# A retention layer and a Gelu MLP on one core: the written-out list of steps in another order, some elementwise steps on other engines, and the Gelu table requested by a step of its own

## The chip, the cores and the metric

The kernel runs on one core of a Trainium2 chip. The core has five engines that each work through their own queue in order: TensorE (PE in the profile, its weight loads PEld), VectorE (DVE), ScalarE (ACT), GpSimd (POOL) and SyncE (SP), which only issues transfers. They meet through semaphores. The metric is the device time of one execution in microseconds. The median of three runs before the change is 296.26 us (296.18 to 296.48).

## What is computed

```
scores = q @ k^T / 8                       # q, k, v: 8 batches, 8 heads, 576 positions, 64 features
D[i,j] = gamma_h ** (i-j) if i >= j else 0 # gamma_h = 1 - 2**(-5-h)
x      = (scores * D) @ v                  # -> x of shape (4608, 512)
h      = x @ w_in                          # (4608, 2048)
g      = 0.5*h*(1 + tanh(c*(h + 0.044715*h**3)))
out    = g @ w_out                         # (4608, 512), float32
```

Inputs and output are float32; the kernel computes its matrix products in float16 with float32 sums.

## The kernel before, in words

The 576 positions of a batch are cut into four chunks of 128 and a tail of 64. A chunk of a batch is a *unit*; there are 40 of them, unit `u` being chunk `u % 5` of batch `u // 5`. The retention is computed chunk by chunk with a running state per head, so a unit needs its own scores, the state left by the units before it, and nothing else. The units 0, 2, 5 and 7 are *wide*: unit 0 stands for the chunks 0 and 1 together, and so on (256 positions at a time, `WIDE`, line 186). The MLP takes 512 positions at a time, `t` = 0 to 8. The first product of a `t` below 6 is made in eight pairs of 128 hidden columns and two halves of 256 positions; from `t` = 6 on, and for the second product from `t` = 1 on, the kernel uses Strassen's scheme of seven products for eight, which takes sums of blocks on VectorE before the matmuls and puts blocks together behind them.

The order of all work is written out by hand: `ORDER` (lines 17 to 123) is a list of 1,332 steps, each a letter with arguments, and the last loop of the kernel (line 1044) issues them one by one. Since the engines run in order, the list sets the order of the instructions within each engine; between the engines only data and buffers decide. The steps of the list that matter here, with the line of the work:

- `L,u,n`: SP loads q, k or v (n = 0, 1, 2) of unit u. For a wide unit it is 512 KB: q as two transfers of 128 runs of 2,048 bytes (line 198), k or v as one of 1,024 runs of 512 bytes (line 203). A tail is two transfers of 256 runs of 256 bytes (line 221), any other unit 1,024 runs of 256 bytes (line 215). All of them wait in one queue of transfers, q1 in the profile.
- `I,g` and `J,g`: POOL issues the load of an eighth of `w_in` or `w_out`, 256 packets that turn float32 into float16 on the way (line 238, queue q0). Hidden columns 0 to 511 need `I` 0 and 1, the next 512 `I` 2 and 3, and so on. `i` and `j` do nothing for these.
- `q`, `k`, `v` (lines 424, 439, 267, 269): float16 copies of a unit's q and v times powers of gamma, and of k. The last letter names the engine: `v` VectorE, `a` ScalarE, `g` GpSimd.
- `D,u` (line 483): q and k of a unit transposed by a transfer; `t,u,q|k,pool` (line 493): the same on TensorE for the first units, and `y` copies the result out of PSUM.
- `X`, `Y`, `m`, `R`, `B`, `x` (lines 619, 636, 644 and 691, 677, 529 to 574, 586 to 599): keys times values, scores, scores times the mask, outputs of a wide unit, the same of other units, and the copy of the output into `xT`, the input of the MLP.
- `a`, `o`, `z` (lines 711 to 731): the running state, its decay, and its float16 copy `sz` for the matmuls.
- `N,t,fc,half` and `F,t,fc,half` (lines 757, 765): eight matmuls of the first product, and their Gelu on ScalarE. `A`, `l`, `f`, `s`, `U` are the same in Strassen's form. `N` and `A` take turns in two PSUM banks, so an `N` waits until the Gelu of the one two places before it has read its bank.
- `O`, `W` and `e`, `V`, `H`, `T`: the second product, and for Strassen's form its sums and its blocks; two other PSUM banks. `S`, `P`, `E`, `Q`: stores of the results, and the last 128 rows in three column parts.
- `K,n`: n matmuls on the identity matrix with no use but to keep TensorE at work (line 1003). `Z`, `g`, `c`: constant tables and zeros.
- `w`: one Gelu of a [128, 1] tile whose result nobody reads (line 1008). ScalarE must load a table when it changes from exponentials to Gelu.

Buffers turn in rings: seven for the loaded pages, four for the float16 q and k, four for the transposed ones, six for `sz`.

Of the kernel before, what the change touches and what calls it, by code (L numbers as in the profile page):

```python
# [28 lines left out]
N,1,4,0 O,0,5 N,1,14,0 F,1,4,0 m,7,0 N,1,2,0 L,12,2 O,0,1 X,7 Y,7,1 F,1,14,0 F,1,2,0 L,15,1 k,9,a  # L29
O,0,6 O,0,2 N,1,10,0 F,1,10,0 q,9,g O,0,3 L,11,2 N,1,6,0 D,9 F,1,6,0 m,7,1 Z,0,g k,11,a a,7,1 O,0,7  # L30
e,0,0,v a,8,1 z,6,1,v O,0,12 T,1,0,v N,1,0,0 e,0,1,a F,1,0,0 z,8,1,g z,7,1,v N,1,8,0 O,0,13 L,10,1
N,1,12,0 R,7 B,9,-1 H,1,0,3,v v,10,v F,1,8,0 x,8 O,0,8 L,11,0 L,12,1 O,0,14 j,5,v F,1,12,0 v,11,v
T,1,1,v q,11 k,10,g x,7 O,0,15 N,1,6,1 H,1,0,1,v L,12,0 D,10 N,1,8,1 O,0,9 F,1,6,1 T,2,0,v v,9,v
O,0,10 e,0,3,a T,3,0,v S,0,0 N,1,14,1 F,1,8,1 H,1,0,2,v m,9 L,14,1 B,10,9 k,12,a D,11 T,2,1,v O,0,11
a,10,0 a,10,1 e,0,2,v N,1,12,1 L,13,2 F,1,14,1 L,13,0 x,9 N,1,10,1 m,10 F,1,12,1 T,3,1,v z,10,0,g
B,11,10 q,12,g W,1,0,1 S,0,3 v,13,v a,11,0 V,1,0,0,a a,11,1 x,10 v,12,v W,1,0,6 L,14,0 F,1,10,1
N,1,2,1 o,11,1 q,13,g F,1,2,1 T,4,0,v D,12 W,1,0,2 L,16,1 V,1,0,1,v N,1,4,1 N,1,0,1 S,0,2 V,1,0,2,a
z,11,0,v F,1,4,1 z,10,1,g j,2,v m,11 S,0,1 N,2,0,0 B,12,11 q,14 a,12,0 H,1,0,4,v k,15,g F,1,0,1
F,2,0,0 W,1,0,7 L,15,0 L,14,2 N,2,8,0 T,4,1,v N,2,4,0 V,1,0,3,v H,1,1,1,v L,13,1 z,12,0,g x,11
k,16,g H,1,1,2,v W,1,0,4 W,1,0,5 F,2,8,0 L,17,0 a,12,1 N,2,6,0 L,17,1 V,1,0,5,v L,19,0 F,2,4,0  # L40
k,13,g D,13 V,1,0,4,v F,2,6,0 m,12 N,2,14,0 v,14,v F,2,14,0 W,1,1,1 z,11,1,g V,1,1,0,a W,1,0,3
V,1,0,6,v L,16,0 N,2,10,0 F,2,10,0 k,14,g W,1,1,6 V,1,1,1,v N,2,12,0 z,12,1,v L,16,2 B,13,12 x,12
L,15,2 v,15,g D,14 q,15 W,1,1,2 H,1,1,3,v m,13 N,2,2,1 V,1,1,2,a W,1,1,7 F,2,12,0 N,2,2,0 V,1,1,3,v
k,17,a W,1,1,4 W,1,1,5 a,13,0 a,13,1 S,1,0 z,13,0,a q,19 q,17 q,16 F,2,2,1 S,1,1 D,15 L,17,2 F,2,2,0
L,18,0 N,2,8,1 B,14,13 N,2,12,1 L,20,0 F,2,8,1 V,1,1,5,v F,2,12,1 N,2,6,1 V,1,1,4,v W,2,0,1 x,13
N,2,10,1 F,2,6,1 m,14 H,2,0,1,v H,2,0,2,v z,13,1,v N,2,0,1 D,16 V,2,0,0,a L,24,1 B,15,14 H,1,1,4,v
a,15,0 L,18,2 H,2,0,3,v W,1,1,3 a,15,1 F,2,0,1 m,15 V,1,1,6,v q,18,g v,17,v F,2,10,1 N,2,4,1
N,2,14,1 L,18,1 L,19,1 x,14 v,16,g F,2,14,1 W,2,0,2 z,15,0,g B,16,15 W,2,0,6 F,2,4,1 x,15 k,19,g
a,16,0 N,3,8,0 V,2,0,1,v V,2,0,2,a a,16,1 F,3,8,0 o,16,1 z,16,0,v m,16 W,2,0,7 D,17 V,2,0,3,v L,23,1
v,18,g N,3,10,0 k,18,g F,3,10,0 L,24,0 L,20,1 N,3,4,0 F,3,4,0 z,15,1,g W,2,0,4 z,16,1,v B,17,16  # L50
L,21,0 N,3,0,0 q,20 V,2,0,5,v a,17,0 L,25,1 L,19,2 D,18 H,2,0,4,v L,20,2 S,1,2 W,2,0,5 N,3,12,0
W,2,1,1 F,3,0,0 m,17 q,21,g H,2,1,3,v V,2,0,4,v H,2,1,1,v F,3,12,0 k,20,g W,2,0,3 N,3,14,0 N,3,6,0
S,1,3 F,3,14,0 V,2,0,6,v V,2,1,0,a L,22,1 N,3,2,0 L,21,1 D,19 H,2,1,2,v W,2,1,6 a,17,1 x,16 z,17,0,g
B,18,17 F,3,6,0 a,18,0 H,2,1,4,v D,20 x,17 a,18,1 W,2,1,2 N,3,8,1 F,3,2,0 m,18 N,3,2,1 i,2,g
z,18,0,a v,19,v V,2,1,2,a L,22,0 W,2,1,7 z,18,1,g V,2,1,1,v F,3,8,1 v,20,g N,3,4,1 F,3,2,1 k,22,v
k,21,v L,25,0 N,3,12,1 W,2,1,5 F,3,4,1 z,17,1,a B,19,18 H,3,0,3,v V,2,1,3,v L,23,0 N,3,0,1 H,3,0,1,v
x,18 F,3,12,1 W,2,1,4 m,19 V,2,1,5,v k,23,g N,3,10,1 W,3,0,1 V,2,1,4,v L,24,2 B,20,19 W,2,1,3
F,3,0,1 L,22,2 x,19 D,21 F,3,10,1 a,20,0 q,23,g N,4,10,0 N,3,14,1 V,3,0,0,a V,2,1,6,v F,4,10,0
H,3,0,2,v W,3,0,6 S,2,0 N,3,6,1 F,3,14,1 S,2,1 F,3,6,1 W,3,0,2 q,22,g a,20,1 L,21,2 D,22 N,4,6,0
m,20 V,3,0,2,a z,20,0,v H,3,0,4,v N,4,12,0 V,3,0,1,v v,21,g L,27,0 F,4,6,0 W,3,0,7 k,24,v B,21,20  # L60
W,3,0,5 N,4,4,0 F,4,12,0 x,20 z,20,1,g V,3,0,3,v H,3,1,3,v W,3,0,4 L,23,2 v,22,v k,25,a v,24,g
a,21,0 V,3,0,4,v m,21 F,4,4,0 S,2,2 N,4,0,0 F,4,0,0 a,21,1 V,3,0,5,v z,21,0,g v,23,g B,22,21 L,28,0
q,25,g N,4,2,0 m,22 L,26,0 x,21 W,3,1,1 q,26,g N,4,14,0 V,3,1,0,a L,30,2 D,23 W,3,0,3 o,21,1 L,27,2
L,26,1 H,3,1,1,v L,26,2 H,3,1,2,v q,24,g W,3,1,2 F,4,2,0 L,29,1 V,3,0,6,v F,4,14,0 V,3,1,2,a N,4,4,1
a,22,0 v,27,v z,22,0,a S,2,3 D,24 W,3,1,6 S,3,0 F,4,4,1 L,28,1 H,3,1,4,v N,4,8,0 z,21,1,v D,25
a,22,1 F,4,8,0 N,4,14,1 W,3,1,7 k,26,a H,4,0,1,v z,22,1,v B,23,22 N,4,6,1 V,3,1,1,v V,3,1,3,v L,25,2
F,4,14,1 a,23,0 W,3,1,5 F,4,6,1 V,3,1,4,v W,3,1,4 N,4,12,1 i,1,g a,23,1 z,23,0,g z,23,1,g F,4,12,1
x,22 W,3,1,3 N,4,0,1 F,4,0,1 q,27 L,28,2 m,23 N,4,2,1 H,4,0,2,v B,24,23 q,28,g N,4,8,1 V,3,1,5,v
F,4,2,1 H,4,0,3,v L,29,0 V,3,1,6,v L,27,1 x,23 F,4,8,1 W,4,0,1 v,25,g N,4,10,1 m,24 V,4,0,0,a D,26
H,4,1,3,v k,28,v F,4,10,1 N,5,2,0 B,25,24 k,27,g S,3,1 F,5,2,0 H,4,1,1,v q,29 a,25,0 L,31,1 a,25,1  # L70
# [1005 lines left out]
```

## Time and profile before

| | |
|---|---|
| median of 3 runs | 296.26 us |
| the profiled execution, first to last instruction (span) | 293.9 us |
| time outside the span, taken against the median | about 2.3 us |
| TensorE at work | 280.3 us, 95% of the span, 4,064 matmuls |
| VectorE, ScalarE, GpSimd at work | 216.6, 150.1, 109.6 us |
| granted TensorE clock, mean | 1.000 |
| read from and written to HBM | 36.70 MB and 9.44 MB |

A page of the profile gives for each engine its busy time, then groups of equal instructions with their mean duration and what ended the idle time before them. The busy time of TensorE is modelled at the ends of its matmuls, so its gaps are read from the starts of successive matmuls. The transfers have a view of their own: for a stretch of time it tells how many packets each queue moved.

### The profile page before, as it was taken

To read this page: it belongs to the slowest core of one execution; us is meant where nothing else is said; L and a number is where in the kernel's file an instruction comes from. 1 tells how busy PE (TensorE), PEld (TensorE's weight loads), DVE (VectorE), ACT (ScalarE), POOL (GpSimd) and SP (SyncE) were. 2 spreads that over 40 slices of the span, in tenths; PEclk is the share of its full clock that TensorE was granted. 3 is DMA by queue.
4 is the path that set the end of the run, shared out by engine and by line. 5 is a ranking of instruction groups with operands and counts; after the bars stand their busy time and mean duration, and the time that the engine had idled before them with its cause. 6 is when DMAs were issued, how large, how long until landed. Compare 5 with 4: busy or idle time off the path is not lost.

```text
span 293.9 us, 9639 instructions
## 1 busy us (share of the span) xinstructions
PE 280.3 (95%) x4064; PEld 235.2 (80%) x4064; DVE 216.6 (74%) x447; ACT 150.1 (51%) x289; POOL 109.6 (37%) x168
## 2 busy tenths in 40 slices
...
GB/s 212 283 236 250 217 220 211 214 179 162 248 142 228 178 186 220 230 206 210 23 235 214 196 166 178 187 204 153 131 195 208 75 205 7 36 8 102 74 25 121
DMA packets 136428, 49.79 MB, mean 169 GB/s; under 512 B 118208, under 2 KB 130880, under 8 KB 136384
## 3 DMA queue, kind: packets, MB, share of 16 engines
...
HBM read 36.70 MB, written 9.44 MB: 157 GB/s over the span
## 4 chain that ended last, share of the span: by engine, by line
PE 86%; POOL 5%; DMA 4%; DVE 3%; issue 1%; ACT 0%; POOLq 0%; ACTq 0%
PE bank L860 30%; PE bank L757 27%; PE bank L957 12%; PE bank L783 6%; DMA w_in_sb<-in_moe_w_in_dram 4%; PE sk L553 2%; PE x L529 2%; POOL w_in_sb L238 2%; PE sk L563 1%; PE x L574 1%; PE bank L987 1%; DVE pages L817 1%; POOL wide L269 1%; PE bank L493 1%; PE x L677 1%
## 5 line engine op out<-in xcount | busy, mean ns | idle before, releaser
L757 PE MATMUL bank<-xT,w_in_sb 128*128 128x256 f16 x768 | 94.4, 273 | 2.1 <-DMA w_in_sb<-in_moe_w_in_dram 2.1
L765 ACT ACTIVATE gT<-bank 128x512 f16<-128x512 f32 x96 | 56.7, 598 | 61.5 <-PE bank L757 59.7
L757 PEld LDWEIGHTS <-w_in_sb 128*128 128x128 f16 x768 | 73.8, 98 | 13.7 <-DMA w_in_sb<-in_moe_w_in_dram 2.7
L860 PEld LDWEIGHTS <-ssum 128*128 128x128 f16 x480 | 46.3, 98 | 6.5 <-issue 0.8
L269 POOL CAST sz<-s 64x256 f16<-64x256 f32 x48 | 24.4, 509 | 66.2 <-DVE s L713 45.9
L860 PE MATMUL bank<-tsum,ssum 128*128 128x256 f16 x360 | 46.0, 273 | 0.6 <-DVE ost L817 0.6
L860 PEld LDWEIGHTS <-gT 128*128 128x128 f16 x360 | 34.8, 98 | 4.5 <-issue 0.2
L424 POOL TENSOR_TENSOR qk<-pages,dec 128x512 f16<-128x512 f32 (+1 forms) x20 | 22.2, 1122 | 32.9 <-DMA pages<-in_q_dram 17.2
L860 PE MATMUL bank<-w_out_sb,gT 128*128 128x256 f16 x240 | 31.1, 273 | 0.0
L817 DVE TENSOR_TENSOR ssum<-gT 128x1024 f16<-128x1024 f16 x30 | 23.9, 798 | 3.9 <-ACT gT L765 3.5
L424 POOL TENSOR_TENSOR v<-pages,dec 128x512 f16<-128x512 f32 (+1 forms) x20 | 20.6, 1030 | 15.3 <-DMA pages<-in_v_dram 10.4
L817 DVE TENSOR_TENSOR ost<-u,bank 128x256 f32<-128x256 f32 x45 | 18.1, 416 | 9.5 <-PE bank L860 9.4
L817 DVE TENSOR_TENSOR ssum<-gT,ssum 128x1024 f16<-128x1024 f16 x30 | 23.4, 782 | 0.2
L691 DVE TENSOR_TENSOR ret<-sk,mask 128x512 f16<-128x512 f32 (+1 forms) x32 | 19.8, 618 | 4.3 <-PE sk L563 4.0
L957 PEld LDWEIGHTS <-pages 128*128 128x128 f16 x192 | 18.4, 98 | 2.8 <-issue 0.3
L957 PE MATMUL bank<-pages 128*128 128x256 f16 x144 | 20.3, 273 | 0.3 <-ACT pages L267 0.3
L783 PE MATMUL bank<-w_out_sb,gT 128*128 128x512 f16 x80 | 19.1, 380 | 0.0
L817 DVE TENSOR_TENSOR u<-u,bank 128x256 f32<-128x256 f32 x30 | 12.4, 415 | 8.7 <-PE bank L860 5.0
L713 DVE TENSOR_TENSOR s<-s,sk 128x256 f32<-128x256 f32 x36 | 14.9, 415 | 5.0 <-PE sk L563 4.0
L593 ACT ACTIVATE xT<-x 128x512 f16<-128x512 f32 (+1 forms) x25 | 14.3, 578 | 8.0 <-PE x L574 8.0
L817 DVE TENSOR_TENSOR hc<-hc,bank 128x512 f32<-128x512 f32 x21 | 14.4, 684 | 5.0 <-PE bank L957 2.3
L267 ACT COPY hc<-bank 128x512 f32<-128x512 f32 x19 | 11.1, 585 | 12.5 <-PE bank L957 12.4
(114 smaller groups left out, 425.8 us busy)
## 6 DMA issues: line engine op xcount, KB each, us to landing
...
```

The costliest lines, as they stand in the source:

```text
L267: nc.scalar.copy(out=o, in_=i)
L269: (nc.vector if eng == "v" else nc.gpsimd).tensor_copy(out=o, in_=i)
L424: eng.tensor_tensor(out=out, in0=s["raw"][:, i, 0:n], in1=dec[:, i // 2, s["j"], 0:n].unsqueeze(2).to_broadcast([128, n, D]), op=ALU.mult,)
L593: nc.scalar.activation(out=xT[:, :, o : o + G * (b - a)].rearrange("c p (h s) -> c p h s", s=G), in_=x[:, a:b].rearrange("c h p s -> c p h ...
L691: nc.vector.tensor_tensor(out=ret[:, :, 0:n], in0=now["two"][:, :, 0, 0:n], in1=mask.unsqueeze(1).unsqueeze(1).to_broadcast([128, 2, n, G] ...
L713: nc.vector.tensor_tensor(out=s32, in0=state[0], in1=kv, op=ALU.add)
L757: nc.tensor.matmul(hps[:, i, :], w_in_sb[:, ct, 128 * (fc + i) : 128 * (fc + i) + 128], xT[:, ct, TB * t % XR + lo : TB * t % XR + hi], st ...
L765: nc.scalar.activation(out=gTs[t][:, fc : fc + TB // (hi - lo), lo:hi], in_=h.pop((t, fc, lo)), func=AF.Gelu_apprx_tanh, bias=0.0, scale=1.0,)
L783: nc.tensor.matmul(ops[t, tcc], gTs[t][:, ft, 128 * tcc : 128 * tcc + 128], w_out_sb[:, ft, :], start=(ft == 0), stop=(ft == NFC - 1),)
L817: (nc.vector if eng == "v" else nc.gpsimd).tensor_tensor(out=out, in0=a, in1=b, op=op)
L860: nc.tensor.matmul(p["ps", bank][:, HN * col : HN * col + HN], a[:, k], b[:, k], start=(k == 0 and i in (1, 6)), stop=(k == HK - 1), skip_ ...
L957: nc.tensor.matmul(p["ps", bank][:, n], w[:, c, 128 * n : 128 * n + 128], x[:, c], start=(n == 0 and c == 0 and i in (1, 2, 5)), stop=(c = ...
```

## The change

All 1,332 steps are still there, with the same arguments but for the engine of some of them, and they stand in another order. Counted over both lists:

- The engine changes in 106 steps. `z`: 31 on GpSimd, 15 on VectorE and 10 on ScalarE become 24, 17 and 15. `k`: 19, 8 and 9 become 13, 7 and 16. `q`: 20 on GpSimd and 16 on VectorE become 15 and 21. `v`: 20 and 16 become 23 and 13. Of `V`, ten move from ScalarE to VectorE (20 and 85 after it), of `l` three net from VectorE to ScalarE (33 and 39), and one or two each of `e`, `E`, `y` and `Z`.
- At the start, the loads of SP stood as k0, q0, v0, k2, q2, v2, k4, q4, q5, k5, v5, v4, k9, k7, q7, v7. They become k0, v0, q0, q2, k2, v2, q4, k4, v4, k5, q5, v5, q7, k7, v7, k9. The loads of `w_in` stood as 2, 7, 1, 0, 3, 6, 4, 5 and become 1, 6, 0, then GpSimd's `c` and `q,2,g`, then 7, 2, 3, 5, 4. Between the first three loads of `w_out` and the other five GpSimd now does `q,7,g`.
- 19 of the 36 filler matmuls of `K` stood ahead of the first transpose; 23 do now.
- `w` stood in the middle of the list, behind 84 of the 96 steps `F`. It now stands behind `z,1,1,a` and ahead of the first `N` and `F`.
- `pair` gives the buffers of a pair of row blocks by the number of the pair in its `t`, not by the count of pairs so far. In both lists the pairs come in turn (0, 1, 0, 1, ...), so each gets the buffers that it had.

```diff
--- before.py
+++ after.py
@@ -15,111 +15,111 @@
 ORDER = """
-L,0,1 Z,1,v L,0,0 I,2,g L,0,2 L,2,1 L,2,0 Z,2,g q,0 k,0,g I,7,g K,4 K,4 K,4 K,3 K,4 t,0,q,h L,2,2
-L,4,1 c t,0,k,h I,1,g v,0,v X,0 y,0,k,v I,0,g I,3,g a,0,1 y,0,q,v Z,3,v k,2,g K,4 K,1 Y,0,1 t,2,k,o
-m,0,1 z,0,1,a I,6,g K,4 Y,0,0 a,1,1 q,2 L,4,0 K,4 t,2,q,h m,0,0 y,2,k,a y,2,q,v I,4,g K,1 R,0 I,5,g
-x,0 Y,2,1 L,5,0 x,1 i,4,v K,3 N,0,2,0 N,0,0,0 g o,1,1 m,2,1 L,5,1 Z,4,g v,2,v F,0,2,0 N,0,12,0 Y,2,0
-F,0,0,0 z,1,1,v N,0,4,0 L,5,2 X,2 k,4,g Z,5,v q,4 F,0,12,0 F,0,4,0 t,4,k,o a,2,1 t,4,q,o a,3,1
-y,4,q,a N,0,8,0 L,4,2 z,2,1,g L,9,1 N,0,10,0 F,0,8,0 k,5,g m,2,0 L,7,1 R,2 F,0,10,0 y,4,k,v B,4,-1
-q,5 x,3 x,2 N,0,14,0 L,7,0 t,5,q,o N,0,0,1 L,7,2 J,1,g F,0,14,0 N,0,6,0 y,5,q,v J,3,g t,5,k,o
-F,0,0,1 m,4 j,1,v J,0,g L,9,0 v,5,v J,2,g L,9,2 F,0,6,0 N,0,8,1 L,10,0 N,0,12,1 k,7,v X,5 y,5,k,a
-F,0,8,1 z,3,1,g F,0,12,1 v,4,v Y,5,0 a,5,1 m,5,0 a,6,1 N,0,4,1 N,0,6,1 F,0,4,1 q,7 F,0,6,1 t,7,k,o
-y,7,k,a N,0,2,1 J,5,g J,4,g N,0,14,1 F,0,2,1 J,6,g L,10,2 B,-1,4 F,0,14,1 x,4 Y,5,1 t,7,q,h y,7,q,a
-J,7,g m,5,1 N,0,10,1 v,7,v F,0,10,1 z,5,1,g R,5 x,5 Y,7,0 o,6,1 x,6 O,0,0 O,0,4 q,10,g L,11,1
...
+Z,2,g j,0,v K,4 K,4 K,3 K,4 K,3 Z,1,g I,1,g K,1 L,0,1 k,0,a L,0,2 K,4 I,6,g t,0,k,h y,0,k,a I,0,g
+v,0,v X,0 L,0,0 q,0 t,0,q,h y,0,q,a K,4 g L,2,0 a,0,1 z,0,1,a a,1,1 Y,0,1 m,0,1 c L,2,1 k,2,v K,4
+L,2,2 q,2,g Y,0,0 m,0,0 L,4,0 t,2,q,h y,2,q,a t,2,k,o y,2,k,v R,0 x,0 L,4,1 x,1 L,4,2 Y,2,1 Z,3,v
+v,2,v o,1,1 z,1,1,a K,1 K,4 w N,0,0,0 F,0,0,0 X,2 m,2,1 N,0,2,0 F,0,2,0 a,2,1 z,2,1,a Y,2,0 I,7,g
+N,0,14,0 F,0,14,0 I,2,g q,4 t,4,q,o N,0,12,0 F,0,12,0 L,5,1 Z,4,g a,3,1 m,2,0 R,2 x,3 k,4,v t,4,k,o
+I,3,g N,0,6,0 Z,0,g I,5,g y,4,q,v x,2 y,4,k,v F,0,6,0 B,4,-1 z,3,1,v N,0,4,0 F,0,4,0 m,4 N,0,12,1
+L,5,0 N,0,6,1 F,0,12,1 v,4,v F,0,6,1 I,4,g N,0,8,1 F,0,8,1 q,5 N,0,10,0 F,0,10,0 N,0,8,0 F,0,8,0
+k,5,g t,5,k,o y,5,k,a L,5,2 v,5,v L,7,0 N,0,0,1 F,0,0,1 Z,5,v L,7,1 J,1,g J,0,g t,5,q,o y,5,q,a
+N,0,14,1 X,5 a,5,1 F,0,14,1 a,6,1 J,2,g Y,5,0 m,5,0 N,0,4,1 F,0,4,1 k,7,a N,0,2,1 F,0,2,1 q,7,g
+B,-1,4 L,7,2 Y,5,1 m,5,1 t,7,q,h x,4 L,9,1 t,7,k,o y,7,k,a z,5,1,g N,0,10,1 F,0,10,1 R,5 x,5 x,6
+y,7,q,v Y,7,0 O,0,4 m,7,0 J,3,g L,9,0 O,0,0 N,1,2,0 F,1,2,0 L,9,2 v,7,v N,1,4,0 Y,7,1 J,5,g o,6,1
+X,7 F,1,4,0 N,1,6,0 F,1,6,0 L,10,0 L,10,2 J,4,g T,3,0,v N,1,14,0 F,1,14,0 O,0,1 q,9 a,7,1 T,1,0,v
+a,8,1 L,10,1 N,1,10,0 L,11,0 F,1,10,0 J,7,g N,1,12,0 k,9,a O,0,5 O,0,6 D,9 J,6,g T,1,1,v T,2,1,v
+O,0,2 N,1,8,0 L,11,1 z,7,1,a F,1,8,0 z,6,1,v F,1,12,0 L,12,1 O,0,7 O,0,3 e,0,0,v e,0,1,a L,13,0
+N,1,0,0 q,10 O,0,12 O,0,13 O,0,14 F,1,0,0 m,7,1 R,7 x,8 H,1,0,3,v v,9,g k,10,g D,10 B,9,-1 v,10,v
...
-W,8,0,5 H,8,0,4,v f,8,3,2 P,2 V,8,0,4,v W,8,0,4 V,8,0,5,v W,8,0,3 O,8,8 E,2,v V,8,0,6,v S,8,0 O,8,9
-O,8,10 O,8,11 P,0 e,8,2,a Q,2 S,8,1 E,0,v P,1 S,8,2 E,1,a Q,0 Q,1 i,7,v
+V,8,0,3,v W,8,0,5 V,8,0,4,v W,8,0,4 V,8,0,5,v W,8,0,3 f,8,2,2 P,2 V,8,0,6,v S,8,0 E,2,v O,8,8 S,8,1
+O,8,9 O,8,10 O,8,11 e,8,2,a S,8,2 P,0 E,0,a Q,2 Q,0 P,1 E,1,a Q,1
 """
...
@@ -834,8 +834,7 @@
         if (t, pr) not in pairs:
             if not tsum:
                 sum_tiles()
-            n = len(pairs)
-            pairs[t, pr] = dict(s=[ssum[4 * (n % 2) + i] for i in range(4)])
+            pairs[t, pr] = dict(s=[ssum[4 * pr + i] for i in range(4)])
         return pairs[t, pr]
 
     def sum_a(t, pr, i, eng):
```

More of the change, by code (lines that the diff above doesn't have):

```diff
@@ L29 @@
[L29 to L70, printed above, removed]
```

138 lines of the change are left out of this document (88 added, 50 removed).

## The prediction

> **What bounds the kernel now.** I read the page's header first, then TensorE's starts in the timeline, then busy time in five stretches.
>
> ```profile
> span 293.9 us, 9639 instructions
> PE 280.3 (95%) x4064; PEld 235.2 (80%) x4064; DVE 216.6 (74%) x447; ACT 150.1 (51%) x289; POOL 109.6 (37%) x168
> ...
> 4.50 5.92 PE L1003 MATMUL bank<-ident 128*128 128x512 f16 x19 [4.50 <-DVE ident L364]
> ...
> 21.30 1.91 PE L757 MATMUL bank<-xT,w_in_sb 128*128 128x256 f16 x16
> 24.85 1.05 PE L757 MATMUL bank<-xT,w_in_sb 128*128 128x256 f16 x8 [1.64 <-DMA w_in_sb<-in_moe_w_in_dram]
> ...
> 41.86 0.45 PEld L493 LDWEIGHTS <-wide 128*128 128x128 f16 x8
> ```
>
> The first `N` starts at 21.30, the next but one waits for `w_in` until 24.85. Two `N` take 1.75 us where nothing waits (the pieces of the chain of waits), so one is 0.873.
>
> ```profile
> core 0: us, PE busy (x) PEld busy (x) DVE busy (x) ACT busy (x) POOL busy (x), PEclk, DMA share, GB/s
> ...
> 21.30:29.28 7.98, 5.88 (x94) 4.41 (x93) 5.50 (x11) 3.70 (x6) 1.01 (x3) 1.00 1.19 249
> 29.28:41.87 12.59, 12.59 (x231) 11.12 (x228) 8.82 (x12) 9.06 (x15) 8.78 (x13) 1.00 1.05 218
> 41.87:224.00 182.13, 182.05 (x2846) 156.03 (x2841) 136.13 (x262) 94.86 (x187) 78.68 (x103) 1.00 0.95 188
> 224.00:229.00 5.00, 3.95 (x35) 3.12 (x33) 4.97 (x9) 3.43 (x7) 2.85 (x3) 1.00 0.81 199
> ```
>
> From 29.28 to 224 TensorE never stops; at 224 to 229 it loses 1 us to a VectorE that is busy for 4.97 of 5. By its starts it waits 2.4 us in all between 29.28 and the end, structural changeovers left out. So the change can win only ahead of 29.28 and in these 2.4 us, and it can lose anywhere. The start is bound by transfers:
>
> ```profile
> q0 software_dynamic: 645, 0.63, 73.9%
> q1 hardware_dynamic: 645, 0.55, 43.0%
> ...
> q1 hardware_dynamic: 997, 0.57, 119.2%
> ...
> q1 hardware_dynamic: 8351, 2.09, 100.8%
> ```
>
> The first two lines are the transfer view for 16 to 21 us: while POOL's queue has weights to move, the two queues move one packet each in turn, 129 per us each. From 36 to 44 us it is 1,119 and 1,114 packets, 140 per us. Alone (7.5 to 9.4 us, packets of 512 bytes) SP's queue moves 997 in 1.9 us, 525 per us; packets of 256 bytes alone (48 to 58) go at 835. So a wide k or v, 1,024 packets, takes 1.5 (27.4 to 28.9 us: 1,021 packets) to 1.95 us alone and 7.3 to 7.9 us beside the weights, and a tail's 512 packets of 64 KB each half cost half as much as a whole wide tensor there.
>
> **The start, step by step.** Loads of SP are issued far ahead, so their order decides.
>
> (1) POOL does two memsets (0.53 each, line 390) ahead of its first `I`, issued at 6.43 before; now at 7.5. The first packets of that queue came 3.3 us after the issue (30 of them in the window 9 to 10); now at 10.8. By then SP's queue, alone at 300 GB/s from 1.9 on, has moved k0, v0, q0, q2 (2.1 MB, 7.0 us) and k2 (1.9).
>
> (2) The 2,048 packets of `w_in` then need 2,048/140 = 14.6 to 2,048/129 = 15.9 us, plus about 0.3 for the gap in which POOL does `c` (1.45, line 395) and `q,2,g`. That multiply is new on POOL; bounds 1.27 (VectorE's, line 439) and 2.4 (twice POOL's 1.20 for half the size); I take 2.2, nearest to POOL's own row. `w_in` ends at 25.7 to 27.2. In that time SP's queue moves as many packets: v2, q4, k4, and little more. Before, it had passed q5 and k5 too, because the weights came in single issues (6.43, 9.03, 11.14) with gaps: 4,014 of its packets against 2,142 from 10 to 28 us.
>
> (3) The matmuls meanwhile. 23 fillers now stand ahead of the first transpose, at 4.50 + 8 x 0.427 + 15 x 0.216 = 11.16 (before: 19, 10.26). The chain from there: `y,0,k` on ScalarE 11.75 to 12.76 (1.01, line 267), `y,0,q` to 13.8, `Y,0,1` at 14.0 (14.75 before), masks 14.5 to 17.9 (2 x 1.22 and a cast of 0.94), `R,0`, `x,0` and `x,1` to 19.75, fillers, first `N` at 20.4, 0.9 earlier. Columns 0 to 511 of `w_in` have landed by 18 (768 packets from 10.8). v2 lands at about 18.9 and holds up VectorE: `v,2`, `o,1,1`, then `z,1,1,a` until 21.5 on ScalarE, and behind it `w` with its table (1.28, the row of line 765) until 23.0. So the request comes too late to hide the table: the first Gelu ends at 23.6 and the third `N` waits 0.8 us. It cost nothing before either, since TensorE stood for `w_in` until 24.85.
>
> (4) Ahead of `t,7,k` the new list has exactly the matmuls that stood ahead of `t,7,q` before (15 `N`, the same `t`, `X`, `Y`, `R`, `B`), and the same ones follow. So 41.87, the old start of that step, is the yardstick. Nothing else waiting, TensorE gets there at 20.4 + 17.7 of work + 0.8 = 38.9: 3.0 us won.
>
> (5) But k7 isn't there. After `w_in` SP's queue still has v4 (0.6 alone), k5 (1.7), q5 (1.8 at 295 GB/s), v5 (1.7), q7, k7. k5 ends at 28.0 to 29.5 and lands 0.7 later (k0: 4.2, landed 4.93). POOL casts it (1.04) and only then issues three loads of `w_out`, whose packets come 2.7 us later, at 32.4 to 33.9. q7 ends at 33.5 to 35, and k7 meets 768 packets of `w_out`: 5.5 to 6 us shared, the rest alone. k7 ends at 38.6 to 41.5 (the upper end if the next five loads follow at once), lands 0.7 later; `k,7,a` on ScalarE is new at this size: bounds 1.01 (its copy of 1,024 in float16) and 1.24 (twice 0.618), I take 1.1. `t,7,k` starts at 40.5 to 43.4; I take 41.7. Queued behind `k,7,a` on ScalarE are `F,0,2,1`, `x,4` and `y,7,k`; TensorE itself waits 2.8 us. Start: 0.2 us won (from 1.4 won to 1.5 lost); the 3.0 are given back. Before, k7 was ahead of `w_out`: VectorE cast it at 35.49, without a wait.
>
> ```profile
> 29.07 1.04 POOL L269 CAST wide<-pages 128x1024 f16<-128x1024 f32 x1
> 30.05 2.88 POOL L238 DMA_DIRECT2D w_out_sb<-in_moe_w_out_dram  x4
> ...
> 35.49 0.94 DVE L269 CAST wide<-pages 128x1024 f16<-128x1024 f32 x1
> ```
>
> v7 and the later `J` have 2 us or more in hand by the same count.
>
> **The engines.** Steps times their rows' means: POOL 108.9 to 94.6, ScalarE 159.4 to 168.9 (with `w`), VectorE 232.4 to 232.6. ScalarE and POOL stay far below 267.3 us of matmuls, so their shares lie beside TensorE's work. VectorE decides by stretch. From `W,4,0,1` to the first `A` of t = 6 it now has 31.5 us of steps to 29.5 of matmuls (before 32.6 to 33.0); around `A,7,0` 16.1 to 13.9 (before 14.5 to 13.1, and there the 1.5 us of waits at 224 to 229 are). Means overlap by 7% (232.4 listed, 216.6 busy), so the two stretches have 29.3 to 29.5, all but full (before 30.3 to 33.0), and 15.0 to 13.9 (before 13.5 to 13.1). What is late next there are `V` and `l`, thus the banks of `W` and `A`. Price: 0.7 more in the second, 0.5 in the first, 1.2 us; bounds: minus 2.4 (all old waits gone) and plus 2.5 (both excesses unhidden). Ten `V` moved to VectorE (0.416 for 0.372) are in these sums. `pair` changes nothing, and the tail (store behind the last copy, 3.1 us) stays.
>
> Sum: 296.26 - 0.2 + 1.2 = 297.2 (the profiled span 293.9 to 294.9; the 2.3 us around it stay).
>
> **Rivals.** (a) k7 comes in time: if POOL's loads of `w_out` start so late, or packets pass so fast alone, that k7 is past by 37. Then 3.0 less 0.5 stay, with 0.5 lost late: 294.3. Against it: k5's landing lets `w_out` go before q7 is through in every count above. (b) The start is even, and VectorE in the late stretches is no worse, since 14.3 us less of POOL stand beside it: 295.3 to 296.6, say 296.0. For it: ssum took 1.42 beside a POOL multiply, 0.69 elsewhere. Against: late POOL steps are the same 18.3 us. (c) TensorE waits so long for k7 that its clock falls. The first eight fillers came 0.42 apart, later ones 0.216: 8 x 0.21 = 1.65 us for a cold engine. A wait of 2.06 us at 11.5 cost nothing (five fillers in 1.25). It needs a longer wait than that; from one of 3.4 us (`t,7,k` at 42.3, 0.6 later than taken) 297.8 + 1.65 = 299.5. The upper third of (5) reaches that far, and a wait of that length need not be enough: 0.12.
> The Trainium skill ("TensorE: Matmul & The Clock Gate", section "What's actually happening") states that the clock halves after an idle window of about 3.4 us; no wait of this trace is long enough to show it, and the row of 2.06 us agrees. By that rule a long wait gives 299.5, without it 297.8.
>
> **How the numbers follow.** Chances: forecast 0.44, (a) 0.17, (b) 0.27, (c) 0.12. No change means within 0.2%, 295.67 to 296.85, about what a measurement can tell. Faster: (a) 0.17 and half of (b), 0.30. Same: 0.12 of (b), 0.05 of the forecast, 0.17. Slower: 0.53. The range, 294.2 to 299.8, takes in (a) and most of (c); the forecast's own is 296.0 to 298.6.
>
> **What would show it.** Right: first `N` at 20 to 20.6, third `N` waiting for a Gelu, TensorE idle 2 to 3.5 us ahead of a transpose (line 493) at 40.5 to 43.4 with ScalarE's cast waiting for k7, then no wait until `W,4`; VectorE full around 165 to 195 and 225 to 240. Wrong: that transpose near 39, or TensorE stopping at places not named.

## The result, and the profile after

The changed kernel takes 304.54 us (median of 4 runs, 302.24 to 306.25) against 296.37 us (4 runs, 296.18 to 297.55): a ratio of 1.026 with a 95% interval of 1.021 to 1.032. A second set of six runs gave 305.17 us. It is slower by about 8 us, far more than the 1 us forecast. Where a run of one variant lies over 1.5% above its fastest, the figures below are of that variant's other runs alone. The page's header and engines:

```profile
span 303.6 us, 9626 instructions
PE 282.8 (93%) x4064; PEld 236.4 (78%) x4064; DVE 217.3 (72%) x455; ACT 159.3 (52%) x302; POOL 95.4 (31%) x147
```

The span has grown by 9.7 us (303.6 against 293.9; the profiled run, 305.61, is one of the longer ones). The matmuls are the same, and VectorE has 0.7 us more to do: the time is waiting. Where, the busy time by stretch shows (stretch, its length, then busy time and count of TensorE, its weight loads, VectorE, ScalarE, GpSimd; granted clock; mean share of the DMA engines; GB/s), first of the changed kernel, then of the kernel before:

```profile
19.60:27.10 7.50, 6.35 (x128) 5.02 (x127) 5.20 (x11) 6.23 (x12) 1.50 (x2) 1.00 1.18 240
27.10:40.25 13.15, 12.77 (x195) 10.72 (x195) 6.49 (x10) 8.70 (x14) 6.45 (x10) 1.00 1.14 250
40.25:101.40 61.15, 61.15 (x865) 48.35 (x866) 38.95 (x68) 32.49 (x63) 20.01 (x26) 1.00 0.99 197
101.40:168.00 66.60, 59.67 (x1000) 52.92 (x998) 46.97 (x99) 32.88 (x64) 20.48 (x25) 1.00 1.03 185
168.00:196.00 28.00, 27.62 (x460) 24.72 (x459) 24.28 (x49) 12.25 (x25) 8.17 (x11) 1.00 0.78 171
196.00:257.00 61.00, 57.43 (x842) 50.03 (x840) 54.34 (x104) 35.89 (x70) 24.47 (x34) 1.00 0.64 131
```

```profile
102.00:168.00 66.00, 65.92 (x1054) 58.61 (x1052) 45.99 (x92) 32.72 (x64) 30.24 (x38) 1.00 1.00 192
196.00:250.00 54.00, 52.95 (x811) 46.82 (x809) 48.90 (x96) 37.53 (x75) 23.60 (x32) 1.00 0.66 143
```

From 40 to 101 us TensorE runs through. Then it is idle for 6.9 of 66.6 us, where the kernel before lost 0.1 of 66.0; and for 3.6 of 61.0 us from 196 on, against 1.1 of 54.0. By the starts of successive matmuls, less each step's usual duration, the waits of over 0.1 us behind 101 us add up like this (a wait is dated here and below by the start of the step that it falls in or follows):

| waits of TensorE | before | after |
|---|---|---|
| start: `t,7,k` (before: `t,7,q`) begins at | 41.87 | 40.25 |
| 101 to 166 us | 0.2 | 7.7 |
| 168 us to the end | 2.2 | 5.9 |

So, before rounding, 1.6 us are won at the start, 7.4 lost in the middle, 3.8 late: 9.6 of the 9.7 us. The start (timeline, one line per run of like instructions: start, length, engine, line, operation, operands, count, in brackets the idle time ahead of it and what ended it):

```profile
19.60 1.04 PE L757 MATMUL bank<-xT,w_in_sb 128*128 128x256 f16 x8
22.70 1.03 PE L757 MATMUL bank<-xT,w_in_sb 128*128 128x256 f16 x8 [0.25 <-ACT gT L765]
27.07 0.83 PE L757 MATMUL bank<-xT,w_in_sb 128*128 128x256 f16 x6 [0.90 <-DMA w_in_sb<-in_moe_w_in_dram]
...
20.66 1.28 ACT L1010 ACT_TABLE_LOAD   x1
39.15 1.04 ACT L267 CAST wide<-pages 128x1024 f16<-128x1024 f32 x1 [0.60 <-DMA pages<-in_k_dram]
...
40.24 0.45 PEld L493 LDWEIGHTS <-wide 128*128 128x128 f16 x8 [0.55 <-ACT wide L267]
```

The first `N` is early, the table load sits nearly hidden under it, `w_in` holds `N,0,6,0` until 27.07, and `t,7,k` does wait for k7's cast, but only 0.55 us. In the middle, the chain of waits (start, length, what) runs through SP's transposes:

```profile
140.90 0.29 PE bank L859 x2
141.19 5.49 DMA qkT<-qk
146.73 0.32 PE sk L563 x16
...
150.77 0.25 PE bank L757 x3
151.03 5.06 DMA qkT<-qk
156.13 0.26 PE sk L563 x8
```

These are `D,23` and `D,24`: TensorE reaches `B,23` at 145.2 and `B,24` at 154.1, and stops 1.06 and 1.70 us in them. Why they are so late, VectorE's timeline tells:

```profile
104.49 0.75 DVE L817 TENSOR_TENSOR ost<-u,bank 128x256 f32<-128x256 f32 x2 [3.66 <-DMA out_dram<-ost]
...
146.87 0.29 DVE L269 CAST qk<-pages 128x256 f16<-128x256 f32 x1 [1.12 <-DMA qkT<-qk]
149.06 0.42 DVE L817 TENSOR_TENSOR ost<-u,bank 128x256 f32<-128x256 f32 x1 [0.68 <-PE bank L859]
149.40 0.42 DVE L424 TENSOR_TENSOR qk<-pages,dec 128x256 f16<-128x256 f32 x1
```

`k,24` takes the tile that unit 23 had, so it stands until `D,23` has landed; `q,24`, whose page landed at 112.6, stands in VectorE's queue behind it and behind a `V` that waits for TensorE; only then can SP issue `D,24`. The first line is another stop, the longest (3.05 us at 101.4): a `V` needs a result tile whose store, `S,0,2`, SP issued at 98.7. The stops look like SP's: late stores, late transposes. That was the first theory.

One number of all units puts it in order. From the issue of `D,u` to the start of `B,u`, units 14 to 31, the kernel before has 9.8 us (median; least 7.8), the changed one 7.0 (least 3.1; six units under 5.5). A transpose lands 4.3 us after its issue (median; 3.7 in the kernel before; up to 5.9). The attention of units 18 to 31 stands 4 to 13 us of matmuls earlier in the changed list (the steps' durations summed over each list up to `B,u`), while the transfers are no earlier: 29.69 MB had moved by 140 us before, 29.63 after. And GpSimd's casts, 42 to 200 us, stand waiting for pages (engine, what for: total, times, longest; before, then after):

```profile
POOL qk L424 <- DMA pages<-in_q_dram: 15.5, 2, 13.1
POOL v L424 <- DMA pages<-in_v_dram: 10.4, 2, 6.6
POOL qk L269 <- DMA pages<-in_k_dram: 1.6, 2, 1.4
```

```profile
POOL qk L269 <- DMA pages<-in_k_dram: 23.4, 4, 9.3
POOL v L424 <- DMA pages<-in_v_dram: 22.5, 5, 9.4
POOL qk L424 <- DMA pages<-in_q_dram: 14.6, 3, 8.1
POOL qk L269 <- DMA pages<-in_q_dram: 4.7, 1, 4.7
```

27.5 us have become 65.2.

### The profile page after: what moved, and what is told of

Its sections match the earlier page's. It is cut to its first block, busy times and chain, and to the rows that moved or that the text cites. A ratio compares the mean times of both kernels' runs of the same rounds, so it can differ in the third digit from the quotient of the medians.

```text
span 303.6 us, 9626 instructions
## 1 busy us (share of the span) xinstructions
PE 282.8 (93%) x4064; PEld 236.4 (78%) x4064; DVE 217.3 (72%) x455; ACT 159.3 (52%) x302; POOL 95.4 (31%) x147
## 4 chain that ended last, share of the span: by engine, by line
PE 37%; DVE 14%; DMA 9%; issue 3%; SPq 1%; ACT 0%; POOL 0%; DVEq 0%
PE bank L859 17%; PE bank L956 8%; DMA qkT<-qk 7%; PE bank L757 6%; DVE ssum L817 3%; DVE pages L817 2%; DVE s L713 1%; DMA pages<-in_v_dram 1%; DVE ost L817 1%; DVE sz L269 1%; DVE ret L691 1%; PE bank L986 1%; PE sk L563 1%; PE bank L783 1%; DVE qk L424 1%
## 5 line engine op out<-in xcount | busy, mean ns | idle before, releaser
L424 POOL TENSOR_TENSOR v<-pages,dec 128x512 f16<-128x512 f32 (+1 forms) x23 | 23.9, 1041 | 38.2 <-DMA pages<-in_v_dram 30.9
L269 POOL CAST sz<-s 64x256 f16<-64x256 f32 x38 | 19.3, 508 | 39.7 <-DVE s L713 30.1
L817 DVE TENSOR_TENSOR ssum<-gT 128x1024 f16<-128x1024 f16 x30 | 22.9, 765 | 0.4 <-ACT gT L974 0.3
L817 DVE TENSOR_TENSOR ssum<-gT,ssum 128x1024 f16<-128x1024 f16 x30 | 22.2, 740 | 0.3
L956 PE MATMUL bank<-pages 128*128 128x256 f16 x144 | 21.2, 273 | 1.1 <-DVE pages L817 0.7
L424 POOL TENSOR_TENSOR qk<-pages,dec 128x512 f16<-128x512 f32 (+1 forms) x13 | 13.6, 1053 | 20.7 <-DMA pages<-in_q_dram 20.3
L267 ACT COPY hc<-bank 128x512 f32<-128x512 f32 x21 | 12.3, 585 | 12.9 <-PE bank L956 12.7
L269 POOL CAST qk<-pages 128x512 f16<-128x512 f32 (+1 forms) x12 | 8.7, 731 | 29.0 <-DMA pages<-in_k_dram 23.4
```

The source lines that it names most:

```text
L267: nc.scalar.copy(out=o, in_=i)
L269: (nc.vector if eng == "v" else nc.gpsimd).tensor_copy(out=o, in_=i)
L424: eng.tensor_tensor(out=out, in0=s["raw"][:, i, 0:n], in1=dec[:, i // 2, s["j"], 0:n].unsqueeze(2).to_broadcast([128, n, D]), op=ALU.mult,)
L817: (nc.vector if eng == "v" else nc.gpsimd).tensor_tensor(out=out, in0=a, in1=b, op=op)
L956: nc.tensor.matmul(p["ps", bank][:, n], w[:, c, 128 * n : 128 * n + 128], x[:, c], start=(n == 0 and c == 0 and i in (1, 2, 5)), stop=(c = ...
```

## The experiments

Times are medians; the kernel before stood between 296.6 and 297.0 us beside them. In the experiments' files the list takes five lines less, so line 262 there is 267 of the changed kernel. The changed kernel's own runs lie 2 to 4 us apart, so differences of under 1.5 us between its variants say little.

| run | us | against the kernel before, 95% |
|---|---|---|
| the changed kernel / once more (e18) | 304.54 / 305.17 | 1.021 to 1.032 / 1.020 to 1.029 |
| e1 store early | 304.68 | 1.021 to 1.034 |
| e2 15 transposes early / e3 both | 314.71 / 311.45 | 1.055 to 1.062 / 1.043 to 1.054 |
| e16 two transposes early / e17 and q casts (five of six runs) | 307.94 / 305.70 | 1.031 to 1.042 / 1.021 to 1.032 |
| e5 few store rows / e6 the same, before | 302.17 / 296.27 | 1.012 to 1.020 / 0.997 to 0.999 |
| e7 before's order / e8 after's order, letters swapped | 306.43 / 341.14 | 1.028 to 1.039 / 1.144 to 1.154 |
| e9 attention later | 316.85 | 1.061 to 1.069 |
| e13 fifth cast tile (two of four runs) / e14 three q casts on GpSimd | 301.80 / 302.86 | 1.012 to 1.022 / 1.017 to 1.028 |
| e10 before, then after / e11 after, then before | 301.10 / 302.18 | 1.009 to 1.019 / 1.011 to 1.019 |
| e4 start of after / e12 longer / e15 longer, `w` late | 295.71 / 294.82 / 295.13 | 0.993 to 0.998 / 0.991 to 0.996 / 0.993 to 0.997 |

### Is it the late store?

```diff
-... N,2,12,0 S,0,3 i,0,a N,2,12,1 ... W,1,1,7 H,1,1,4,v S,0,2 B,14,13 ...
+... N,1,12,1 S,0,3 H,1,0,1,v ... W,1,0,2 S,0,2 N,1,4,1 ...
```

> The changed list with two steps moved alone: S,0,3 and S,0,2 (stores of the first token block's results) stand about 6 us of matmuls behind the copies e,0,3 and e,0,2 that fill them, instead of 28. Theory A (the 3.05 us stop of TensorE ahead of product W,2,0,1 is a result buffer waiting for S,0,2, which SP issues only at 98.7): that stop is gone, 304.5 falls by about 3 to 301.5 (300.5 to 302.5), and VectorE has no wait for a store near 101. Rival B (VectorE and the banks are the limit from here on, the store only the last to come): the stop stays, or comes back a few steps later, and the time stays within 1 us of 304.5.

304.68 us: no gain. The stop at 101.4 is gone, but now ScalarE stands for a page 12 us ahead of it, and TensorE 2.15 and 0.77 us behind ScalarE's Gelus (timeline, ScalarE, then TensorE):

```profile
90.63 0.62 ACT L262 CAST qk<-pages 128x512 f16<-128x512 f32 x1 [3.19 <-DMA pages<-in_k_dram]
91.16 0.59 ACT L760 ACTIVATE gT<-bank 128x512 f16<-128x512 f32 x1
...
91.80 1.03 PE L752 MATMUL bank<-xT,w_in_sb 128*128 128x256 f16 x8 [1.99 <-ACT gT L760]
```

The page is k14's: SP issued `L,14,1` at 86.87 instead of 84.18. But the changed kernel run once more (e18, below) has the same stops, 1.80 and 0.77 us, and none at 101, with both stores in their old places and `L,14,1` at 85.15 (its timeline):

```profile
91.23 1.03 PE L757 MATMUL bank<-xT,w_in_sb 128*128 128x256 f16 x8 [1.64 <-ACT gT L765]
```

So the stop at 101.4 comes and goes without an edit, and no gain hangs on it; that the store's move delayed the page is not shown.

### Is it the late transposes?

```diff
-... q,14,g ... D,12 v,12,g B,12,11 ... V,3,0,4,v F,4,6,0 L,29,0 q,24 ... U,3,1 D,24 B,24,23 ...
+... k,12,g D,12 q,14,g ... v,12,g B,12,11 ... q,24 D,24 N,4,4,1 ... U,3,1 B,24,23 ...
```

> The changed list with 15 of the 31 DMA transposes D moved forward, to 4 to 6 us of matmuls ahead of the attention step B that reads them (as they stand, eight are right ahead of it), never ahead of their own casts; nothing else. Theory A (a late transpose in SP's queue stops TensorE at line 563): the stops at 145.2, 154.1, 224.2 and 244.1 (1.06, 1.70, 0.63, 0.60) go, TensorE's waits for qkT fall from 3.8 us to under 1, and the time falls by 3 to 4 to about 301 (300 to 302). Rival B (VectorE is the limit from 140 on: what TensorE no longer waits for a transpose it waits for VectorE's banks): the waits at line 563 go but those at lines 859 and 956 grow, the time stays above 303. Rival C (SP stands at the early transposes, loads and stores behind them come later): new waits for pages or ost, 304 or more.

> Both moves together. Theory A: the gains add, 304.5 - 3 - 3.5 = 298 (297 to 299.5); what stays above the kernel before is VectorE's stops of the late stretch. Rival B: no more than the better one of the two alone, 301 or more.

314.71 and 311.45 us: 10 and 7 us worse. Waits at line 563 fell from 3.8 to 1.1 us as expected, but SP now stands at transposes whose casts aren't done (from 18.1 to 26.2 us at casts of q on VectorE alone), the loads behind them come later, and `B,31` starts at 203.0 instead of 192.3. Now the same with only two moved:

```diff
-... L,27,2 D,22 B,22,21 ... v,23,v D,23 B,23,22 ... q,24 N,4,4,1 ... U,3,1 D,24 B,24,23 ...
+... L,27,2 D,22 D,23 B,22,21 ... v,23,v B,23,22 ... q,24 D,24 N,4,4,1 ... U,3,1 B,24,23 ...
```

> The changed list with two of its transposes moved alone: D,23 forward right behind D,22, and D,24 right behind q,24; 4 and 14 steps of TensorE's and other engines' order stand as they were. Theory (the stops at 145.2 and 154.1 are these two, standing in SP's queue behind loads that could wait): D,23 is issued near 136 instead of 141.2 and lands before B,23; k,24 does not wait, q,24 is cast at 148, D,24 issued at once and landed by 153; the stops 1.06 and 1.70 lose 2 to 2.5 us, 302 to 302.6. Rival G (the queue is full, so what goes ahead of the loads takes their place: their pages come later, and the stop comes one or two units on): 304 or more, with a stop at B,25 to B,28.

307.94 us, the rival. The stops at 145.2 and 154.1 go; 0.70 us come at `B,22` and 0.90 at a product that waits for a `V` of ScalarE. And SP, free earlier, comes to `D,24` early and stands there 4.7 us for `q,24`; `L,27,0` behind it is issued at 157.7 instead of 155.7. VectorE reaches `q,27` and has no page, and TensorE waits for the state that VectorE was to make next (timeline, VectorE, TensorE):

```profile
163.48 1.46 DVE L419 TENSOR_TENSOR qk<-pages,dec 128x512 f16<-128x512 f32 x1 [3.74 <-DMA pages<-in_q_dram]
164.86 0.41 DVE L708 TENSOR_TENSOR s<-s,sk 128x256 f32<-128x256 f32 x1
...
165.32 0.43 PE L548 MATMUL sk<-v,qk 64*64 64x64 f16 x16 [3.34 <-DVE s L708]
```

Behind that stop the granted clock fell (stretches of the same run, columns as above; the last but two is the granted clock):

```profile
160.00:165.00 5.00, 1.99 (x22) 1.69 (x19) 1.52 (x2) 1.96 (x5) 4.18 (x5) 0.90 1.03 138
165.00:167.00 2.00, 1.60 (x52) 1.38 (x53) 2.00 (x5) 0.77 (x2) 1.27 (x2) 0.50 0.38 74
167.00:169.00 2.00, 2.00 (x12) 1.39 (x11) 1.43 (x5) 0.82 (x2) 0.00 (x0) 0.50 0.45 90
171.00:174.00 3.00, 3.00 (x78) 2.70 (x76) 1.98 (x6) 1.45 (x4) 0.14 (x1) 1.00 1.42 199
```

By an estimate from these rows, some 5.5 us of work at 0.50 cost up to 2.7 us more. In e2 the stop at 101 grew to 4.65 us and the clock was at 0.50 from about 106 to 112.5, and again from 146.8 to 150.2.

### Is it bytes, the four cast tiles, or VectorE's casts?

In e5 and e6 the 12 stores write 8 of 128 rows:

```diff
-        stores[t, tcc] = out[r0 : r0 + 128, :], ost
+        few = 8 if (t, tcc) in FEW else 128
+        stores[t, tcc] = out[r0 : r0 + few, :], ost[0:few]
```

> The changed kernel with 12 stores (S,0,2, S,0,3, all of blocks 1 and 2, S,3,0 and S,3,1; issued from 86 to 178 us) writing 8 of their 128 rows; 120 rows of each of these tiles are left unwritten. Every instruction keeps its place and its wait; 2.95 of 49.8 MB are not moved. Theory T (the DMA engines are full, share 1.0, until 168 us, and the changed list puts the attention steps of units 18 to 31 earlier by 4 to 13 us of matmuls than the list before, so their pages and transposes come too late): 2.9 MB are 14 us of transfer at 205 GB/s, spread over 90 us, so the pages land 2 to 14 us sooner and most of the 6.4 us of stops between 101 and 160 goes: 304.6 falls by 4 to 7, to 298 to 300.5. Theory Q (SP stands at a store or a transpose and all behind it waits, bytes do not matter): within 1.5 us of 304.6. Theory V (VectorE is the limit from 100 on): within 1.5 us too, with the waits at lines for the banks grown.

> The kernel before with the same 12 stores writing 8 of 128 rows. All theories: TensorE has no wait over 0.25 us between 42 and 223 there, so within 0.5 us of the kernel before, 296.4 to 297.4. It is the control: a gain of more than 1 us here would say that the shorter stores help by another way than pages that come sooner.

302.17 us, 2.4 less than the changed kernel and short of the 4 to 7 expected; the control gains 0.5. The 3.05 us stop goes and 1.65 come at 88.7 and 90.4, as 2.57 do in e18 without any edit; those at 145.2 and 154.1 shrink to 0.49 and 1.23. Bandwidth is a part at most: about 2 MB less in stores by 140 us let the other transfers run only some 0.3 MB ahead.

```diff
-ring(sb, [128, 2 * H, D], F16, "qk16", "qk16", 4)
+ring(sb, [128, 2 * H, D], F16, "qk16", "qk16", 5)
...
-        return halves[turn[0] % 5]
+        return halves[turn[0] % 4]
```

> The changed kernel with five tiles in turn for the cast q and k (qk16) instead of four; to make room for it, the late products A have four scratch tiles for their sums instead of five. Same instructions, same order. Theory R (a loop of unit to unit: k,24 takes the tile of unit 23, whose transpose D,23 is issued at 141.2 and lands at 146.7, so VectorE stands 1.12 us at k,24, q,24 behind it is cast at 149.4 though its page landed at 112.6, D,24 is issued at 151.0 and TensorE stops 1.70 us at 154.1): with a fifth tile k,24 takes another unit's, the stop at 154.1 goes and the next ones shrink; the attention of unit 31 begins 1.5 to 3 us sooner than 192.3, and the time is 301.5 to 303.5 (the fewer scratch tiles may give back up to 1 us behind 196). Rival F (SP's queue of transfers in flight alone is late): unit 31 begins within 0.7 us of 192.3, and the time is 304 or more.

Two runs at 300.65 and 302.94 us, some 3 us under the changed kernel, as theory R had it, and two at 305.19 and 307.52: too far apart to tell whether the tile gains. With four scratch tiles some late groups of `A` add up values that the next group has overwritten; the instructions are the same. In the kept run, the 300.65 one, `B,31` begins at 188.2 instead of 192.3; of the stop at 101.4 it has 0.40 us, and of those of e18 at 88.6 and 91 only 0.23. `k,24` no longer waits, but the stop that the tile was to take away is still there (timeline, VectorE's `k,24` and `q,24`, then the weight load of `B,24`):

```profile
142.49 0.80 DVE L264 CAST qk<-pages 128x256 f16<-128x256 f32 x1
145.78 0.42 DVE L419 TENSOR_TENSOR qk<-pages,dec 128x256 f16<-128x256 f32 x1
...
152.38 0.14 PEld L558 LDWEIGHTS <-qkT 64*64 64x64 f16 x8 [1.62 <-DMA qkT<-qk]
```

`q,24` is cast at 145.78, and SP, busy with `D,25` and a load, issues `D,24` at 148.1. The Trainium skill ("Perfetto Trace Analysis", section "Optimization Strategy") says that the same gap repeating on the engine that should be full can mean too few buffers. Here the trace differs: the buffer's wait went (1.12 us to none), TensorE's stop stayed (1.57 us by the starts, 1.70 before).

```diff
-... q,34 ... q,35 ... q,36 ...
+... q,34,g ... q,35,g ... q,36,g ...
```

> The changed kernel with three casts of the late stretch, q,34, q,35 and q,36, on GpSimd instead of VectorE; nothing else. The chain that ended last runs through VectorE without a gap from 194.3 to 203.9, with q,34 (0.85 us at 202.2) in it, and SP's D,35 waits for q,35, cast at 219.4. Theory V (VectorE is the limit there): the stops at 200.9, 202.2 and 224.2 (2.4 us) lose about 1 us, 303 to 304, minus up to 1 more. Rival (the long casts on GpSimd come later still, behind its waits for pages): 304.5 or more.

> The two transposes moved, and q,34, q,35 and q,36 on GpSimd. Theory: the gains add, 304.5 - 2.2 - 1.7 = 300.6 (300 to 301.5). Rival G: the q casts' gain alone, 302.5 to 303.5.

302.86 us, 1.7 less; and 305.70, 2.2 less than e16. Less both times, though the runs overlap. In both traces the stop at 202.2 falls from 0.84 to 0.31 and the one at 224.2 goes: VectorE does hold up the late stretch. But the gain of the two transposes, which e17 was to add to, was a loss.

### Order or engines?

```diff
-L,0,1 Z,1,v L,0,0 I,2,g L,0,2 L,2,1 L,2,0 Z,2,g q,0 k,0,g I,7,g ... y,0,k,v I,0,g I,3,g a,0,1 y,0,q,v ...
+L,0,1 Z,1,g L,0,0 I,2,g L,0,2 L,2,1 L,2,0 Z,2,g q,0 k,0,a I,7,g ... y,0,k,a I,0,g I,3,g a,0,1 y,0,q,a ...
```

This is the list before with the changed list's letters (e7); e8 is the other way about.

> The order of the list before, with the engine letters of the changed list (106 steps have another engine). Theory T (the order alone makes the loss): within 1.5 us of the kernel before, 296 to 298.5. Rival E (the casts on other engines make it, GpSimd's long casts v above all): 300 or more.

> The order of the changed list, with the engine letters of the list before. Theory T: the stops between 101 and 165 stay, 302 to 307. Rival E: they go, 299 or less. If both e7 and e8 are slow, each order fits only its own letters, and neither part alone is the cause.

306.43 and 341.14 us. Each order runs better with its own letters: the old order with the new engines loses 9.7 us with stops spread over the run (2.94 us at 51.5, 1.58 at 96.4, 1.46 at 152.2 the largest three), and the new order with the old engines takes 36.6 us more than with its own. Neither part alone is the cause. And e7's transposes have a lead of 10.0 us: a good lead alone doesn't make a fast kernel.

Then the whole attention was put later against the products, in the changed list:

```diff
-... D,23 B,23,22 z,22,1,g k,25,a ... V,3,0,3,v z,23,0,a V,3,0,4,v F,4,6,0 L,29,0 q,24 N,4,4,1 H,3,0,4,v W,3,0,4 ...
+... V,3,0,3,v V,3,0,4,v F,4,6,0 N,4,4,1 H,3,0,4,v W,3,0,4 ... D,23 B,23,22 z,22,1,g k,25,a ... z,23,0,a L,29,0 q,24 ...
```

> The changed list with two of its streams shifted against each other: the steps of the attention (L, q, k, v, D, B, m, a, o, z, x, in their own order and on their own engines) stand 2.6 to 7.9 us of matmuls later between the attention of unit 19 and that of unit 31, so that hidden layers and products (N, F, H, W, V) come ahead of them, as far as N's inputs allow; before and behind that, nothing is moved. Theory L (the changed list asks for the attention of units 18 to 31 earlier, by 4 to 13 us of matmuls, than casts, pages and transposes can have it ready; the lead from the ready transpose to the step that reads it is under 0.5 us there at units 14, 18, 20, 22, 23 and 24): most of the stops at 125, 137, 145, 154 and 166 (4.6 us) go, and 304.5 becomes 300 to 302. Rival (the order is good and something else late, VectorE or the engines' letters): 303.5 or more.

316.85 us: this theory fell too. The lead rose to 8.7 us and waits at line 563 fell to 2.0, but now the products wait: 10.2 us at line 859 (854 in that file) between 42 and 290 (6.3 in the changed kernel), with `V` behind casts and sums on VectorE, the longest 2.74 us, until 174.3.

### Which stretch?

The list can be spliced where both lists have done nearly the same matmuls: what a list has not done by then follows in the other's order.

```diff
-... D,32 z,31,0,g A,6,0,5 B,32,31 ...
+... D,32 A,6,0,7 B,32,31 i,4,v i,1,g k,34,v W,5,0,6 q,33,g A,6,0,5 ...
```

So e11 goes on behind `B,32,31`; e10 is the same with the lists exchanged. e4 and e12 leave the changed list at the start, e15 moves `w`:

```diff
-... N,0,10,1 F,0,10,1 R,5 x,5 x,6 y,7,q,v Y,7,0 O,0,4 m,7,0 J,3,g ...
+... N,0,10,1 F,0,10,1 i,4,v J,3,g j,1,v L,9,0 L,9,2 L,10,0 J,5,g ... y,7,q,a J,7,g v,7,v R,5 ...
...
+... N,0,10,1 F,0,10,1 R,5 x,5 x,6 y,7,q,v Y,7,0 i,4,v J,3,g j,1,v L,9,0 ...
...
-... K,1 K,4 w N,0,0,0 F,0,0,0 ... F,5,0,0 z,26,0,g ...
+... K,1 K,4 N,0,0,0 F,0,0,0 ... F,5,0,0 w z,26,0,g ...
```

> The list before up to B,32,31 (at 200 us), then the remaining steps as the changed list has them. Theory: the changed list's stops behind that point (3.9 us, against 2.2 in the kernel before) and the waits at VectorE's banks are its share of the late stretch, so 296.8 + 1.7, 298 to 299.5. Rival (the late stretch costs only because the middle leaves debts): 297 or less.

> The changed list up to B,32,31 (at 207 us), then the remaining steps as the list before has them. Theory: start and middle of the changed list alone: 304.5 - 1.7, 302 to 303.5. Rival (the late stretch holds more than the stops show): under 301.

> The changed list up to F,0,10,1 (the 150 steps of its start), then all remaining steps in the order and with the engines of the list before. Theory A (the changed start is a gain of 1.6 us, from t,7,k at 40.25 against 41.87, and all of the loss lies in the order behind it): 296.3 - 1.6 = 294.7 (294.2 to 295.4), faster than both. Rival D (the start is paid for later: w_out's loads J, which it issues later, and the pages pushed back by them hold up the rest): 296 or more, with TensorE stopping at O or W steps for w_out_sb or at B steps for pages.

> As the run with the changed start and the rest of before, but with the changed list kept for four more steps (R,5, x,5, x,6, y,7,q on VectorE, Y,7,0), because in that run TensorE stopped 0.98 us ahead of Y,7,0 for the copy y,7,q, which stood behind k,7's copy on ScalarE. Theory: the stop goes, 295.7 - 0.9, 294.8 (294.3 to 295.3). Rival: VectorE is late for v,7 instead, and the stop comes at R,7 or X,7: 295.5 to 296.

> As the best run (the changed start with four more steps, the rest of before), but with the step w back at its place of the list before, behind F,5,0,0, so that the first real Gelu of F,0,0,0 has to wait for its table. Theory: the table's 1.28 us come back on ScalarE behind the first N, two banks deep, and TensorE stops about 1.3 us near 22 as it did in the kernel before; part of it is hidden by the wait for w_in at 26 (1.0 to 1.3 us), which is fixed by the transfer: 294.8 + 0.3, 294.8 to 295.4. Rival W (the early table is most of the gain of the start): 296 or more.

e4, 295.71 us: the changed start alone gains 1.2 us (0.5 to 2.1). e11, 302.18: start and middle cost 5.3, so the middle 6.5; it reaches to `B,32,31`, at 207 us of the changed kernel, and so takes in 2.2 us of stops that the table above counts as late. e10, 301.10: the late stretch alone costs 4.3, not the 1.7 expected, with stops of 1.43 and 2.20 us at 202 and 204. The kept run, 303.93, is the longest of e10's four (the shortest is 300.13), and behind the second stop the granted clock is 0.50 for 3.4 us, some 1.6 us more by the starts of the steps there; the changed kernel has no such fall. Together the parts would be 9.6; the changed kernel loses 8.2, so middle and late stretch overlap, or part of e10's stops comes from the joint. e12, 294.82, is the fastest: 0.7% under the kernel before (0.4 to 0.9), since `y,7,q` on VectorE takes away the 0.98 us stop that e4 had at 41.2. With `w` late it is 295.13; the two intervals overlap, so the early table is worth 0.3 us or nothing that can be told. The start gains by the rest of its changes, its loads and casts among them, which were not taken apart.

> The changed kernel itself once more, beside the two others: its four runs lay between 302.2 and 306.3, four times as far apart as those of the kernel before, so 303 to 305.5 as a median; differences of under 1.5 us between its variants mean little.

305.17 us (303.53 to 305.72), with stops of 1.80 and 0.77 us at 88.6 and 91 in place of the one at 101.4. The changed kernel's single stops move from run to run. Their sum hardly does: 8.9 us from 41 to 168 us and 4.7 behind, against 7.7 and 5.9 in the first profile. The middle is the larger part both times.

## Why the prediction was wrong

Right, but in the main by luck: the direction, since most of the loss fell where the sum has no term. Right in the start: first `N` 19.60 (forecast 20.4), `w_in` until 27.07 (25.7 to 27.2, though the terms given add up to 27.0), `q,2,g` 1.90 us (2.2), third `N` 0.25 us behind a Gelu (0.8), and the yardstick of equal matmuls: TensorE ready for `t,7,k` at 39.7 (38.9), ScalarE's cast waiting for k7.

Mis-sized: step (5), "k7 isn't there". It was there at 39.15, 1.6 us before the middle of the count, so `t,7,k` began at 40.25 and not 41.7, 1.6 us won and not 0.2. GpSimd's cast of k5 began at 25.60, not 28.7 to 30.2, because SP's queue had more time alone than steps (1) and (2) gave it. The first packet of `w_in` came at 11.86, not 10.8 (SP's queue moved 568 from 10.8 to 11.8), and v2 landed at 13.0 and not 18.9; and between the third and the fourth load of `w_in` GpSimd's queue was empty for 1.8 us (no packet from 17.4 to 19.2, the sum had 0.3), in which SP's moved 1,254 packets.

Mis-sized: the late stretches, 1.2 us with a bound of 2.5. TensorE's waits behind 168 us grew by 3.8: by 2.2 up to `B,32,31` and by 1.6 behind it. Spliced in alone, that last part costs 4.3 (e10), joint and clock included. The step compared VectorE's sums with TensorE's over whole stretches; the larger stops are 0.5 to 0.9 us each; at two of them single casts of q stood ahead of what TensorE needed, as e14 showed.

Failed: "then no wait until `W,4`". The sum has no term between `t,7,k` and `W,4,0,1`, and that is where 7.4 us went (6.5 by splicing, up to `B,32,31`). The prediction counted every moved step by its duration and each engine's total, and SP's and GpSimd's queues up to 43 us. Of the moved `D`, `S`, `L` and casts behind that it asked only whether the engines had room, not when each transfer would be issued and how long before its reader. The lists alone show a difference: eight `D` stand less than 0.5 us of matmuls ahead of their `B` in the changed one, three before. It is a sign and no remedy, since moving `D` forward made the kernel slower (e2, e16).

Of the rivals, (a) came nearest for the start and none named the middle. (c), the clock, did not happen: the longest stop was 3.05 us and the granted clock stayed at 1.00. It did happen in e16 behind 3.34 us and in e2 behind 4.65, but also in e10 behind 2.04, and in e2 it did not behind 3.28. The rule of the Trainium skill that the prediction weighed ("TensorE: Matmul & The Clock Gate", section "What's actually happening", an idle window of about 3.4 us), read as the length of one stop, agrees with e2's 4.65 and 3.28 and nearly with e16, and not with e10.

Shown: the loss is in the middle and late, and it is waits only. Taking away one wait in the middle did not bring it back: with the stores forward the time stays, with a transpose forward SP stands until its cast, with a fifth tile the transpose behind it is still late, with the attention later the products wait. Argued only: why. The likeliest reading is that in the middle pages, casts, transposes and products of neighbouring units follow each other with less lead than before (for the transposes 7.0 us against 9.8), and every engine is in order, so that whatever is late has something needed behind it. Against lead as the whole account stand e7 and e9, which have 10.0 and 8.7 and are slow. Which of the list's many moves makes the waits stays open, and no repair of the changed middle was found; what helped was to put the old one back.
